# Changing the first feed-forward product of a two-layer attention network to a seven-product scheme, and moving the second bias into PSUM

## The chip, the cores and the metric

The kernel runs on one core of one Trainium2 chip. The metric is the device time of one execution in microseconds (us). One core has no second die to compare with, so the state of a run is told from its granted clock and from the spread of its times.

The engines are TensorE (PE, whose weight loads are listed as PEld), VectorE (DVE), ScalarE (ACT), GpSimd (POOL) and SyncE (SP, which here issues nearly all DMA).

## The reference

Two layers, each with windowed attention and a feed-forward part (FFN), over 2048 tokens of width 1024. The two layers use the same weights.

```python
def _A_ref(x, wqkv, wo):      # 32 heads of 32; each token sees 8 keys: itself and
    ...                       # those 2, 4, ... 14 positions back
    logits = jnp.einsum("bhsd,bhswd->bhsw", q, kg) * scale
    attn = _softmax(logits, axis=-1)
    o = jnp.einsum("bhsw,bhswd->bhsd", attn, vg)
    return o... @ wo
def _B_ref(x, w1, b1, w2, b2):    # w1 1024 x 3584, w2 3584 x 1024
    h = jnp.einsum("bsd,df->bsf", x, w1) + b1
    r = jnp.where(h > zero, h, zero)
    return jnp.einsum("bsf,fd->bsd", r * r, w2) + b2
for _ in range(2):
    x = x + _A_ref(_layernorm(x), A_wqkv, A_wo)
    x = x + _B_ref(_layernorm(x), B_w1, B_b1, B_w2, B_b2)
```

Inputs and weights are bf16; the only intermediate that matters here is `h`, which is formed by the first FFN product (FFN1).

## The kernel before

Tokens are worked in blocks of 512; four blocks and two layers make eight block steps, simply called blocks here. In each block PE does the q, k and v projections (`pq`), the output projection (`py`), FFN1 (`ph`), FFN2 (banks `X`, `Y`, `Z`) and a few sums over heads (`lg`). A small planner in the program orders the operations and assigns buffers; attention of the next block runs on DVE while PE does the FFN of this one.

FFN1 is plain: 28 output chunks of 8 matmuls with 512 columns each. ACT then takes the bank with bias and relu, and squares it.

```python
def SF1(self, u):
    for g in range(F // 512):
        wt = self.weights(self.w1_v[:, :, g * 512:(g + 1) * 512], KD)
        for cc in range(4):
            f = g * 4 + cc
            def fm(...):
                for kd in range(KD):      # KD = 8
                    nc.tensor.matmul(ph[:], wt[:, kd, cc * 128:(cc + 1) * 128], xnT[:, :, kd, :], start=(kd == 0), stop=(kd == KD - 1))
            def fr(...):
                nc.scalar.activation(out=r[:], in_=ph[:], func=ACTF.Relu, bias=self.b1T[:, f:f + 1], scale=1.0)
            def fs(...):
                nc.scalar.activation(out=r2[:, f, :], in_=r[:], func=ACTF.Square)
    ...
```

FFN2 already uses a seven-product scheme in three banks. Its combined weights (`tw`) are formed once on DVE in the first block and stored to DRAM; its raw weights come straight from the input `B_w2`. The bias b2 is added by DVE:

```python
# in SW, after the output projection and layernorm of each 128-token tile
nc.vector.tensor_tensor(xm[:], xm[:], self.b2b[:], ALU.add)
```

The softmax here doesn't subtract the row's maximum and nothing guards it: scores larger than these inputs give would overflow.

Of the kernel before, what the change touches and what calls it, by code (L numbers as in the profile page):

```python
# [15 lines left out]
W = 8  # L16
# [11 lines left out]
def dve(n, fast=True):  # L28
    return 0.15 + n * (0.000523 if fast else 0.00104)
# [170 lines left out]
class _Kernel:  # L200
# [19 lines left out]
    def setup(self):  # L220
        Buf.count.clear()
        nc, tc, ctx = self.nc, self.tc, self.ctx
        D, KF = self.D, self.KF
        const = ctx.enter_context(tc.tile_pool(name="const", bufs=1))
        nc.scalar.preload_act_table_set("natural_log_exp_and_others")
        self.ident = const.tile([128, 128], BF, name="ident")
        nc.vector.memset(self.ident[:], 1.0)
        nc.gpsimd.affine_select(out=self.ident[:], in_=self.ident[:], pattern=[[-1, 128]], compare_op=ALU.is_equal,
                                fill=0.0, base=0, channel_multiplier=1)
        self.grp = const.tile([128, H, 4], F16, name="grp")  # L230
        nc.vector.memset(self.grp[:], 1.0)
        nc.gpsimd.affine_select(out=self.grp[:], in_=self.grp[:], pattern=[[-4, H], [0, 4]], compare_op=ALU.is_ge,
                                fill=0.0, base=0, channel_multiplier=1)
        nc.gpsimd.affine_select(out=self.grp[:], in_=self.grp[:], pattern=[[4, H], [0, 4]], compare_op=ALU.is_ge,
                                fill=0.0, base=3, channel_multiplier=-1)
        self.mask01 = const.tile([128, W, HALO], F32, name="mask01")
        nc.vector.memset(self.mask01[:], 1.0)
        nc.gpsimd.affine_select(out=self.mask01[:], in_=self.mask01[:], pattern=[[-1, W], [1, HALO]],
                                compare_op=ALU.is_ge, fill=0.0, base=0, channel_multiplier=0)
        self.eps = const.tile([128, 1], F32, name="eps")  # L240
        nc.vector.memset(self.eps[:], EPS)
        self.b1T = const.tile([128, KF], F32, name="b1T")
        with nc.allow_non_contiguous_dma(reason="tiny bias load"):
            nc.gpsimd.dma_start(self.b1T[:], self.b1.rearrange("(c p) -> p c", p=128))
        self.b2b = const.tile([128, D], BF, name="b2b")
        nc.gpsimd.dma_start(self.b2b[:], self.b2.rearrange("(o d) -> o d", o=1).to_broadcast((128, D)))

        self.wqkv_v = self.wqkv.rearrange("(kt p) n -> p kt n", p=128)
        self.wo_v = self.wo.rearrange("(p c) n -> p c n", c=self.NCH)
        self.w1_v = self.w1.rearrange("(kt p) n -> p kt n", p=128)  # L250
        self.w2_v = self.w2.rearrange("(kt p) n -> p kt n", p=128)
        x2d = self.x if len(self.x.shape) == 2 else self.x.rearrange("b s d -> (b s) d")
        o2d = self.out if len(self.out.shape) == 2 else self.out.rearrange("b s d -> (b s) d")
        self.x_par = x2d.rearrange("(a two) d -> two a d", two=2)
        self.out_par = o2d.rearrange("(a two) d -> two a d", two=2)
        self.xs = [tc.dram_tile([self.S, D], F32, name=f"xs{l}") for l in range(self.n_layers - 1)]
        self.T = {"T1": 0, "T2": 1, "T3": 2, "T4": 3}
        self.B = {"B11": (0, 0), "B21": (1, 0), "B22": (1, 1)}
        self.tw = [tc.dram_tile([128, KF // 2, BLK], F16, name=f"tw{i}") for i in range(4)]
        self.xnd = [tc.dram_tile([self.S, D], BF, name=f"xnd{l}{h}") for l in range(self.n_layers) for h in "AB"]  # L260

        p = self.p
        self.arena = ctx.enter_context(tc.tile_pool(name="arena", bufs=1))
        self.psum = ctx.enter_context(tc.tile_pool(name="psum", bufs=1, space=PSUM))
        sizes = [("8K", 12, 8320), ("4K", 16, 4096), ("r2", 1, KF * BLK * 2), ("2K", 4, 2048), ("1K", 4, 1024),
                 ("H", 8, 128), ("s", 12, 32)]
        for c, n, b in sizes:
            p.classes[c] = (n, b)
        p.classes["ps"] = (8, 2048)
        p.caps.update(w=5, xt=2, P0=5, P1=5, pr=2, dn=1, pb=2, xm=8, xnA=1, xnB=1, s1=1, tw=4, xn=2, xo=2, q=1, k=1, v=1, o=1, e=1, r2=1)  # L270
# [12 lines left out]
    def dma(self, out, src, r, w, mb, prio=None, after=(), name="dma"):  # L283
        def fn():
            self.nc.sync.dma_start(out(), src())  # L285
        return self.p.add("SP", 0.08, fn, r, w, self.nxt() if prio is None else prio, after, mb=mb, name=name)
# [23 lines left out]
    def combine_group(self, j0, n):  # L310
# [3 lines left out]
        for k2 in range(2):  # L314
            for n2 in range(2):
                t = b[k2, n2] = Buf("4K", "tw", [128, step, BLK], F16)
                self.dma(lambda t=t, n=n: t[:, :n].bitcast(BF), lambda k2=k2, n2=n2, j0=j0, n=n: self.w2_block(k2, n2)[:, j0:j0 + n, :],
                         (), [(t, 0)], n * 0.131, name="twl")
# [25 lines left out]

    def ln(self, x, xv, xcells, xnT, tl, scr, key, prio, vec, on_pe=False):
        nc, p, D, KD = self.nc, self.p, self.D, self.KD
        xn = Buf("2K", "xn", [128, D], BF)
# [27 lines left out]
        else:  # L375
# [4 lines left out]
            def f2():  # L380
                nc.scalar.activation(out=xn[:], in_=xv(), func=ACTF.Square, bias=nmean(), scale=1.0, accum_out=s2())
                nc.scalar.activation(out=lnv(), in_=s2(), func=ACTF.Ln, bias=self.eps[:], scale=1.0 / D)
                nc.scalar.activation(out=rstd(), in_=lnv(), func=ACTF.Exp, scale=-0.5)
                nc.scalar.activation(out=nmr(), in_=nmean(), func=ACTF.Identity, scale=rstd())
            p.add("ACT", 1.3, f1, xr, [(xn, 0), (sm, 0)], prio, name="ln1")
            p.add("ACT", 1.8, f2, xr + [(sm, 0)], [(xn, 0), (sm, 1)], prio - 0.1, name="ln2")
# [10 lines left out]
    def ln_first(self, x, xv, xnT, tl):  # L397
        nc, p, D, KD = self.nc, self.p, self.D, self.KD
        xn = Buf("2K", "xn", [128, D], BF)
# [26 lines left out]
    def transpose(self, xn, xnT, tl, prio):  # L426
        nc, p, KD = self.nc, self.p, self.KD
        pt = Buf("ps", "pt", [128, KD, 128], BF)

        def f5():  # L430
            for kd in range(KD):
                nc.tensor.transpose(pt[:, kd, :], xn[:, kd * 128:(kd + 1) * 128], self.ident[:])

        def f6():
            nc.vector.tensor_copy(xnT[:, tl], pt[:])
        p.add("PE", 1.0, f5, [(xn, 0)], [(pt, 0)], prio, name="pt")
        p.add("DVE", 0.69, f6, [(pt, 0)], [(xnT, tl)], prio - 200.0, name="ptc")
# [12 lines left out]
    def SA(self, u):  # L450
        layer, b = divmod(u, self.NB)
        st = self.state.setdefault(u, {})
        xnT = Buf("8K", "xnA", [128, 4, self.KD, 128], BF)
# [11 lines left out]
    def SQ(self, u, jobs, order=None):  # L465
# [9 lines left out]
        for nm in jobs:  # L475
            st[nm] = Buf("8K", nm, [128, NCH, offs[nm] + BLK], F16)
# [12 lines left out]
        for nm, c0 in order:  # L489
# [3 lines left out]
            def fm(pq=pq, w=w, c0=c0):  # L493
                for kd in range(KD):
# [4 lines left out]
                  [(pq, 0)], [(dst, c0)], 2.0, name="cast")  # L499
# [7 lines left out]
    def S2(self, u, depths):  # L507
# [10 lines left out]
        def prod(hb):  # L518
# [5 lines left out]
            for c in range(NCH):  # L524
# [15 lines left out]
                if lvl == depth:  # L540
                    def fl(cur=cur, i=done):
                        for j in range(W // 2):
                            nc.tensor.matmul(lg[j][:], self.grp[:].rearrange("p h r -> p (h r)"), cur[:, 2 * j:2 * j + 2, :],  # L543
                                             start=(i == 0), stop=(i == nleaf - 1))
                    self.pe(4, fl, [(cur, 0)], [(g, 0) for g in lg], prio=-1.0, name="lg")
# [4 lines left out]
        def expo(hb):  # L550
            e = es[hb] = Buf("8K", "e", [128, W, HB], F32)
# [5 lines left out]
        def norm(hb):  # L557
            e = es[hb]
            t = Buf("4K", "dn", [128, W // 2, HB], F32)
            ri = Buf("1K", "ri", [128, HB], F32)  # L560
# [19 lines left out]
            p.add("DVE", dve(2048, False), f2, ec + [(ri, 0)], [(pb, 0)], self.nxt(), name="pb")  # L580

        def av(hb):
            pb = pbs[hb]
            for c in range(NCH):
# [10 lines left out]
                p.add("DVE", dve(1024) + dve(512) + dve(256), f2, [(pr, 0)], [(pr, 0), (o, (c, hb))], self.nxt(), name="avt")  # L595
# [10 lines left out]
    def SW(self, u):  # L606
# [5 lines left out]
        xnT = st["xnB"] = Buf("8K", "xnB", [128, 4, KD, 128], BF)  # L612
        wos = [self.weights(self.wo_v[:, :, g * 512:(g + 1) * 512], KD) for g in range(D // 512)]
        st["xm"] = []
        for tl in range(4):
            t = b * 4 + tl
            x, xv = self.load_x(layer, t, [st.get("gatek")])
            xm = Buf("4K", "xm", [128, D], F32)
            for db in range(D // 512):
# [7 lines left out]
                def fe(py=py, xm=xm, xv=xv, db=db):  # L627
# [5 lines left out]
                    (("xnd", 2 * layer + 1, t), 0), 1.0, True, on_pe=(u == 0))  # L633
            p.add("DVE", dve(1024, False), lambda xm=xm: nc.vector.tensor_tensor(xm[:], xm[:], self.b2b[:], ALU.add),
                  [(xm, 0), (xm, 1)], [(xm, 0), (xm, 1)], self.nxt(), name="b2")

    def SF1(self, u):
# [24 lines left out]

    def SF2(self, u):
# [17 lines left out]
        def mul(name, left, lcells, banks, start):  # L681
            for half in range(2):
                w = self.w2_rhs(name, half)
                for q in range(2):
                    def fm(w=w, q=q, half=half):
                        for j in range(g):
                            jj = half * g + j
                            nc.tensor.matmul(banks[q][:], left(jj, q), w[:, j, :], start=(start and jj == 0), stop=(jj == h - 1),  # L688
                                             skip_group_check=True)
                    self.pe(g, fm, lcells(half * g) + [(w, 0)], [(banks[q], 0)], name="pp")  # L690
# [24 lines left out]
        mul("B21", *block(1, 0), Y, True)  # L715
# [5 lines left out]
        mul("T1", lambda jj, q: s1[:, jj, q * 128:(q + 1) * 128], lambda j0: [(s1, j0)], Z, True)  # L721
# [11 lines left out]
        mul("T4", *block(1, 1), X, False)  # L733
# [15 lines left out]
    def build(self):  # L749
# [11 lines left out]
        for u in range(NU):  # L761
# [12 lines left out]
            self.SF1(u)  # L774
# [53 lines left out]
```

## Time and profile before

| | before |
|---|---|
| time, median of 15 runs (range) | 1235.25 us (1233.72 to 1237.5) |
| profiled span, granted clock | 1233.3 us, 0.997 |
| PE busy / idle | 1204.0 / 29.3 us |
| DVE, ACT busy | 962.2 us (78%), 614.5 us (50%) |
| DMA | 311.6 MB, 253 GB/s |

The prediction used three runs, with a median of 1236.23 us.

First, parts of the page of the kernel before: busy time by engine with its share of the span and the number of instructions, the chain of work that ended last, and the groups of FFN1. In a group line stand busy time, mean ns of one instruction, and the idle time of the engine just before them.

```profile
PE 1204.0 (98%) x5549; PEld 615.9 (50%) x5588; DVE 962.2 (78%) x1283; ACT 614.5 (50%) x1097; POOL 4.1 (0%) x10
...
PE 87%; DVE 7%; DMA 2%; SPq 2%; ACT 1%; issue 1%; ACTq 0%; DVEq 0%
...
L652 PE MATMUL ph<-xnB,w 128*128 128x512 bf16 x1792 | 389.4, 379 | 0.0
...
```

PE is the bound: it is busy 98% of the span and holds 87% of the chain. FFN1 is the largest group, 389 us, and PE never waits in it (0.0 us). The mean of 379 ns is the length of one pipelined matmul; the pace is found by dividing a stretch by its count, which gives 215.8 ns (146 matmuls issue in 31.5 us from 454.54).

The waits of PE in the kernel before (total us, times, longest) show what the idle time at the start is made of. `xn` is the output of layernorm; `pt` are its transposes on PE; `xnA` is the transposed input of the projections, brought by DMA from its copy `xnd` in DRAM; `w` is any weight buffer:

```profile
PE pt L432 <- ACT xn L418: 9.2, 3, 8.2
PE pq L496 <- DMA xnA<-xnd0A: 4.5, 1, 4.5
PE pt L432 <- ACT xn L352: 3.0, 4, 1.6
PE py L624 <- DVE o L593: 2.3, 1, 2.3
PE pq L496 <- DMA w<-in_A_wqkv_dram: 1.7, 1, 1.7
```

### The profile page before, as it was taken

What the parts mean: (1) busy time and instruction counts of PE and PEld (TensorE: products, weight loads), DVE (VectorE), ACT (ScalarE), POOL (GpSimd) and SP (SyncE); (2) the same over time, 40 slices, a digit from 0 to 9 for tenths busy, and PEclk for the clock granted to TensorE, in tenths of its full rate; (3) what the DMA queues carried; (4) which work ended last, traced back from release to release, by engine and by line L of the source; (5) the groups of instructions that cost most, each with busy time, mean ns of one, the idle gap of its engine ahead of it and who ended that gap; (6) DMA issues with size and microseconds to landing.
All of it is one profiled execution on the core that took longest, in us unless ns stands there. A gap on an engine that the chain in (4) does not pass through costs nothing.

```text
span 1233.3 us, 14702 instructions
## 1 busy us (share of the span) xinstructions
PE 1204.0 (98%) x5549; PEld 615.9 (50%) x5588; DVE 962.2 (78%) x1283; ACT 614.5 (50%) x1097; POOL 4.1 (0%) x10
## 2 busy tenths in 40 slices
PE   6988999999999999999999999999999999999998
PEld 3554544555445644456444564455544555444443
DVE  4999999998993989939897498957989399994032
ACT  6632793158901697027950379404892135721740
POOL 1000000000000000000000000000000000000000
PEclk9999999999999999999999999999999999999999
DMA  9776967977498874978759876697849976449915
GB/s 319 263 208 215 357 196 237 378 230 257 146 330 317 248 233 154 352 258 273 248 196 344 311 223 218 250 346 242 271 131 325 353 219 208 159 132 362 355 48 195
DMA packets 252327, 311.63 MB, mean 253 GB/s; under 512 B 69920, under 2 KB 197920, under 8 KB 252256
## 3 DMA queue, kind: packets, MB, share of 16 engines
q1 hardware_dynamic: 240512, 295.73, 71.3%
q10 hardware_dynamic: 8064, 14.68, 3.4%
q0 software_dynamic: 3680, 0.28, 0.5%
q8 instruction: 44, 0.72, 0.2%
q14 instruction: 27, 0.22, 0.0%
HBM read 261.36 MB, written 34.60 MB: 240 GB/s over the span
## 4 chain that ended last, share of the span: by engine, by line
PE 87%; DVE 7%; DMA 2%; SPq 2%; ACT 1%; issue 1%; ACTq 0%; DVEq 0%
PE ph L652 30%; PE pq L496 21%; PE X L688 15%; PE py L624 8%; PE Z L688 8%; PE Y L688 4%; SPq L285 2%; DVE pr L588 2%; PE lg L543 1%; DMA xt<-in_A_x_dram 1%; DVE P L528 1%; DVE pr L591 1%; DMA w<-tw 1%; DVE pr L592 1%; DVE tw L324 1%
## 5 line engine op out<-in xcount | busy, mean ns | idle before, releaser
L652 PE MATMUL ph<-xnB,w 128*128 128x512 bf16 x1792 | 389.4, 379 | 0.0
L496 PE MATMUL pq<-xnA,w 128*128 128x512 bf16 x1536 | 341.8, 382 | 7.0 <-DMA xnA<-xnd0A 4.5
L496 PEld LDWEIGHTS <-w 128*128 128x128 bf16 x1536 | 220.8, 144 | 123.2 <-issue 10.6
L652 PEld LDWEIGHTS <-w 128*128 128x128 bf16 x1792 | 175.4, 98 | 211.1
L688 PEld LDWEIGHTS <-r 128*128 128x128 f16 x1344 | 131.5, 98 | 159.5 <-issue 1.0
L688 PE MATMUL X<-w,r 128*128 128x512 f16 (+1 forms) x888 | 197.0, 379 | 1.2 <-DMA w<-tw 0.8
L655 ACT ACTIVATE r<-ph,b1T 128x512 f16<-128x512 f32 x224 | 152.1, 679 | 59.3 <-PE ph L652 53.9
L498 ACT CAST k<-pq 128x512 f16<-128x512 f32 x64 | 37.0, 588 | 286.5 <-PE pq L496 285.7
L528 DVE TENSOR_TENSOR P<-q,k 128x2048 f16<-128x2048 f16 x128 | 151.4, 1223 | 12.2 <-ACT q L498 12.2
L588 DVE TENSOR_TENSOR pr<-pb,v 128x2048 f16<-128x2048 f16 x128 | 156.4, 1222 | 0.6
L658 ACT ACTIVATE r<-r 128x512 f16<-128x512 f16 x224 | 141.0, 629 | 6.9
L536 DVE TENSOR_TENSOR P<-P,P 128x2048 f16<-128x2048 f16 x99 | 121.2, 1225 | 2.7
L624 PE MATMUL py<-w,o 128*128 128x512 bf16 x496 | 113.1, 383 | 3.1 <-DVE o L593 2.3
L591 DVE TENSOR_TENSOR pr<-pr 128x1024 f16<-128x1024 f16 x128 | 88.4, 690 | 3.8
L624 PEld LDWEIGHTS <-o 128*128 128x128 bf16 x512 | 50.4, 99 | 63.6 <-DVE o L593 2.9
L498 ACT CAST q<-pq 128x512 f16<-128x512 f32 x64 | 37.3, 583 | 41.8 <-PE pq L496 38.9
L592 DVE TENSOR_TENSOR pr<-pr 128x512 f16<-128x512 f16 x128 | 54.4, 425 | 4.4
L577 DVE TENSOR_TENSOR pb<-e,ri 128x2048 f16<-128x2048 f32 x16 | 36.7, 2291 | 26.3 <-ACT ri L574 26.3
L742 DVE TENSOR_TENSOR xo<-X,xm 128x512 f32<-128x512 f32 (+1 forms) x32 | 22.0, 688 | 43.4 <-PE X L688 41.9
L352 ACT ACTIVATE xn<-xm,sm 128x1024 bf16<-128x1024 f32 x32 | 39.7, 1242 | 32.2 <-DVE sm L370 32.2
L504 DVE COPY halo<-k 128x56 f16<-128x56 f16 x8 | 1.4, 177 | 68.7 <-ACT k L498 68.7
L679 DVE TENSOR_TENSOR s<-r 128x1792 f16<-128x1792 f16 x16 | 17.3, 1082 | 46.8 <-ACT r L658 46.8
(68 smaller groups left out, 820.3 us busy)
## 6 DMA issues: line engine op xcount, KB each, us to landing
w<-in_B_w_dram SPq DMA_DIRECT2D x56, 1024.0 KB, 8.1
w<-tw SPq DMA_DIRECT2D x64, 896.0 KB, 8.4
w<-in_A_wqkv_dram SPq DMA_DIRECT2D x48, 1024.0 KB, 9.7
w<-in_B_w_dram SPq DMA_DIRECT2D x48, 896.0 KB, 6.9
w<-in_A_wo_dram SPq DMA_DIRECT2D x16, 1024.0 KB, 9.0
xt<-xs SPq DMA_DIRECT2D x32, 512.0 KB, 9.1
xs<-xo SPq DMA_DIRECT2D x32, 256.0 KB, 6.7
xt<-in_A_x_dram SPq DMA_DIRECT2D x28, 256.0 KB, 7.5
```

The lines of the kernel that those rows point to most:

```text
L496: nc.tensor.matmul(pq[:], wv[:, kd % 4, c0:D:8], xnT[:, :, kd, :], start=(kd == 0), stop=(kd == KD - 1))
L498: p.add("ACT", act(512), lambda dst=dst, c0=c0, off=off, pq=pq: nc.scalar.copy(dst[:, c0, off:off + BLK], pq[:]), [(pq, 0)], [(dst, c0)], ...
L528: nc.vector.tensor_tensor(cur[:], q[:, c, None, hb * HB:(hb + 1) * HB].to_broadcast([128, W, HB]), _win_ap(k[:, c, :], HALO + hb * HB, HB) ...
L536: nc.vector.tensor_tensor(other[:], other[:], cur[:], ALU.add)
L588: nc.vector.tensor_tensor(pr[:], pb[:], _win_ap(v[:, c, :], HALO + hb * HB, HB), ALU.mult)
L591: nc.vector.tensor_tensor(pr[:, 0:4, :], pr[:, 0:4, :], pr[:, 4:8, :], ALU.add)
L592: nc.vector.tensor_tensor(pr[:, 0:2, :], pr[:, 0:2, :], pr[:, 2:4, :], ALU.add)
L624: nc.tensor.matmul(py[:], o[:, c, tl * 128:(tl + 1) * 128], wos[db][:, c, :], start=(c == 0), stop=(c == NCH - 1))
L652: nc.tensor.matmul(ph[:], wt[:, kd, cc * 128:(cc + 1) * 128], xnT[:, :, kd, :], start=(kd == 0), stop=(kd == KD - 1))
L655: nc.scalar.activation(out=r[:], in_=ph[:], func=ACTF.Relu, bias=self.b1T[:, f:f + 1], scale=1.0)
L658: nc.scalar.activation(out=r2[:, f, :], in_=r[:], func=ACTF.Square)
L688: nc.tensor.matmul(banks[q][:], left(jj, q), w[:, j, :], start=(start and jj == 0), stop=(jj == h - 1), skip_group_check=True)
```

## The change

The intent is to save PE work: FFN1 of blocks 2 to 8 is cut into 2 x 2 sub-blocks and computed with seven products in place of eight. A product is 8 matmuls of 256 columns. Seven products for each of seven steps make 392 matmuls of 256 columns in a block, where 224 of 512 stood. Half as many columns cost about half the time, so this is 7/8 of the work.

What pays for it:

- Combined weights. Seven groups of sums of w1 are formed on DVE during block 1 and stored to DRAM (`w1s`); blocks 2 to 8 load them, 7/4 as many bytes as plain w1.
- Combined activations: eight small DVE subtractions per block (`T`).
- Three PSUM banks per step (256 columns of the lower and 256 of the upper half of `h`; there are seven steps, worked two by two). Products 1, 6, 7 and 4 are summed one after another in bank X, and after each of the first three ACT must copy X away (`u`) before the next product may add to it. DVE then adds the copies to banks Y and Z, and adds bias and relu.
- To give DVE room, b2 moves into PSUM as a ones-by-b2 matmul inside FFN2 (6 per block, of 512 columns each), layernorm statistics move from DVE to ACT, and the softmax weights become bf16.

The diff also holds smaller matters: activations in f16 in place of bf16, differently cut buffer pools (14 of 4 KB in place of 16, for one), other priorities in the planner.

The diff, cut to its core:

```diff
-    def SF1(self, u):
+    def SF1_plain(self, u):        # kept for block 1
...
+    PAIR = [(0, 1), (1, 1), (0, 5), (1, 5), (0, 6), (1, 6), (0, 2), (0, 7), (1, 2), (1, 7), (0, 4), (0, 3), (1, 4), (1, 3)]
+    LAST = [(0, 1), (0, 5), (0, 2), (0, 6), (0, 7), (0, 4), (0, 3)]
+    def combine_w1_group(self, dp, after):
+        ...    # 4 raw loads, 4 DVE sums, 7 stores to self.w1s per group
+    def ffn1_step(self, r2, dp):
+        X, Y, Z = (Buf("ps", nm, [128, 2, HB], F32) for nm in "XYZ")
+        def keep(i):
+            p.add("ACT", act(512), lambda: nc.scalar.copy(us[i][:], X[:]), [(X, 0)], [(us[i], 0)], 1.0, name="u")
+        def mul(pr, w, wi, rhs, rc):
+            bank = {1: X, 6: X, 7: X, 4: X, 2: Y, 5: Z, 3: Z}[pr]
+            ...
+                for a in range(2):
+                    for k in range(4):
+                        nc.tensor.matmul(bank[:, a, :], lw[:, k, a * 128:(a + 1) * 128], rhs(k), ...)
+            ...    # 1, 6, 7: keep(); 2, 7, 3: DVE adds a copy to Y or Z, then bias and relu; square on ACT
...
-            p.add("DVE", ..., nc.vector.tensor_tensor(xm[:], xm[:], self.b2b[:], ALU.add), ...)
+                        if b2 is not None and half == 0:
+                            nc.tensor.matmul(banks[q][:], self.ones[:], self.b2r[:, b2 * BLK:(b2 + 1) * BLK], start=start, stop=False, ...)
...
-                    (("xnd", 2 * layer + 1, t), 0), 1.0, True, on_pe=(u == 0))
+                    (("xnd", 2 * layer + 1, t), 0), 1.0, False, on_pe=(u in (0, self.NU - 1)))
-            self.SF1(u)
+            (self.SF1 if u else self.SF1_plain)(u)
```

`PAIR` is the order in which the products of two steps are interleaved, as (step, product); `LAST` is the order of the seventh step, which stands alone.

## The prediction

> **What bounds it now.** TensorE. The page gives PE 1204.0 of 1233.3 us busy (98%) at granted clock 0.997. From the second of the eight token blocks on, the chain of waits is almost only matmuls; a block takes 147.6 us (FFN1 starts at 290.7, 438.3, 585.9 us): 192 pq + 64 py + 224 ph + 196 FFN2 + 8 lg = 684 matmuls of 512 columns, 0.2158 us each. Of the idle 29 us, 8 lie before the first transpose, 15 up to 133 us, 0.3 in each block. DVE is 78% busy, ACT 50%, DMA about 76%.
>
> **What changes.** FFN1 of blocks 2 to 8 becomes a seven-product (Strassen-like) scheme: per block 392 matmuls of 256 columns for 224 of 512.
>
> PE:
> - The Trainium skill ("TensorE: Matmul & The Clock Gate", Back-to-back issue gap) gives 262 cycles for 256 columns, 109 ns. The trace agrees as far as it can: eight 128-column transposes with their own weight loads issue some 57 ns apart, which with 215.8 ns at 512 interpolates to an estimated 110 ns. So weight loads should stay hidden. FFN1 goes from 48.35 to about 43.1 us: 7 x 5.2 = -36.6 us.
> - b2 moves from DVE into PSUM: 6 matmuls per block, 48 x 0.2158 = +10.4.
> - The last block's xnB is transposed on PE: 32 more, +2 to 3.
> - Net about -24 us, all on the critical path.
>
> DVE, per middle block (now 118.8 us busy in the stretch 382 to 530): removed b2 add 4.7, bn statistics about 7, pb in bf16 about 2. Added 21 adds out of PSUM at 0.69 (14.4; the skill, "VectorE: DVE Perf Modes", tier table: a PSUM operand keeps tensor_tensor at 1x, as 685 ns for xm shows), 28 small bias/relu (about 7), 8 half-block differences of 0.425 (3.4). Estimate 130 of 143 us. One-off: 28 weight combinations, about 19 us, in blocks 1 and 2.
>
> ACT: layernorm statistics move here, +2.8 us for each of 32 tiles; FFN1 epilogue 36.6 to about 33 per block.
>
> DMA: FFN1 weights per block from 7.2 to 12.8 MB in larger packets: that stretch goes from 190 to some 310 GB/s, about what FFN2 draws already (326 GB/s, with 0.3 us of PE idle). Forming the combinations adds 20 MB before about 290 us, where DMA is already 72 to 94% busy.
>
> **Critical path.** PE stays the bound, with little slack elsewhere: DVE has some 9 us per block before the next py waits for o; in FFN1 PE leaves ACT about 1.7 us to copy the X bank, and other ACT instructions take up to 1.25 us. I expect 0 to 1.5 us of new PE idle per block, and a few us near the start.
>
> **Prediction.** 1236 - 24 + 3 = **1215 us**, range 1200 to 1233. Chances: faster by over 2% (below 1211.5) 0.42, within 2% 0.55, slower 0.03.
>
> **What the profile would show.** Right: FFN1 matmuls 109 to 111 ns apart; steady block 143 to 145 us; PE 96% or more busy; DVE near 86%; the gain almost all in blocks 2 to 8. Wrong on the matmul: FFN1 well above 43 us with PEld near full. Wrong on slack: PE waiting in FFN1 for ACT copies or combined weights, or py for o.
>
> **What would make it wrong.** Weight loads not hidden at 256 columns; DMA saturation through FFN1 and FFN2; DVE falling behind; combined weights late for block 2. On the other side: less idle time at the start than now.

## More of the kernel before

Nearly all loads, the stores of results and the transposes of activations go into one SP queue (only the stores of layernorm outputs, `xnd`, are issued by ACT, and a few small loads by GpSimd); it works in order: a load whose buffer is not yet free holds up what stands behind it.

Next, the windows view of the kernel before. A line gives a stretch and its length in us, then the busy time of PE, PEld, DVE, ACT and POOL, the granted PE clock, the share of the 16 DMA engines' time that packets took (it can pass 1, since packets overlap), and GB/s. The first three lines split the run at the first output projection of block 2 and of block 7; the last three are FFN1, FFN2 and the projections of one middle block.

```profile
0.00:248.21 248.21, 224.05 (x1036) 120.99 (x1042) 222.23 (x299) 125.01 (x232) 4.08 (x10) 0.99 0.83 272
248.21:986.36 738.15, 736.83 (x3397) 378.74 (x3421) 594.56 (x787) 387.30 (x700) 0.00 (x0) 1.00 0.77 260
986.36:1233.30 246.94, 243.15 (x1120) 116.13 (x1127) 145.40 (x198) 102.20 (x165) 0.00 (x0) 1.00 0.64 210
438.20:487.70 49.50, 49.50 (x230) 22.44 (x230) 43.74 (x55) 45.63 (x82) 0.00 (x0) 1.00 0.60 191
487.70:529.80 42.10, 41.94 (x194) 19.16 (x195) 34.97 (x53) 1.63 (x3) 0.00 (x0) 1.00 0.93 329
529.80:585.80 56.00, 55.89 (x260) 34.08 (x260) 39.90 (x50) 30.11 (x57) 0.00 (x0) 1.00 0.78 264
```

Length less PE busy is PE's idle time: 24.2 us at the start, only 1.3 us over five whole blocks, 3.8 us at the end. So in the middle there is nothing to gain but PE work.

## The result, and the profile after

| | before | changed |
|---|---|---|
| time, median (range, runs) | 1235.25 us (1233.72 to 1237.5, 15) | 1233.3 us (1230.47 to 1236.18, 12) |
| profiled span, granted clock | 1233.3 us, 0.997 | 1233.8 us, 0.993 |
| PE busy / idle | 1204.0 / 29.3 us | 1183.9 / 49.9 us |
| DVE busy | 962.2 us (78%) | 1037.2 us (84%) |
| ACT busy | 614.5 us (50%) | 670.2 us (54%) |
| DMA | 311.6 MB, 253 GB/s | 368.2 MB, 298 GB/s |

The ratio to the kernel before is 0.9982, with a 95% interval of 0.997 to 0.9994. Ratios are the mean time of one kernel's fast runs over that of the other's of the same rounds, so they are not quite the ratios of the medians quoted. Executions over 1.5% slower than the fastest of the same kernel are left out of the means. The change gains about 2 us where 21 were forecast. The changed kernel's times fall into two groups, six from 1230.5 to 1232.6 us and five from 1235.5 to 1236.2, with one at 1234.0 between. The profiled run (1235.5) lies in the upper group, which is why the spans do not show even those 2 us. Why there are two groups is not known, and a wait seen in this one profile need not be in every run.

The page of the changed kernel, the same parts:

```profile
PE 1183.9 (96%) x6798; PEld 736.5 (60%) x6844; DVE 1037.2 (84%) x1556; ACT 670.2 (54%) x1240; POOL 4.0 (0%) x10
...
PE 70%; DVE 9%; ACT 9%; DMA 7%; SPq 2%; issue 1%; ACTq 0%; DVEq 0%
...
L787 PEld LDWEIGHTS <-w 128*128 128x128 f16 (+1 forms) x2520 | 246.3, 98 | 46.9 <-issue 10.3
...
L787 PE MATMUL X<-T,w 128*128 128x256 f16 x1120 | 137.5, 273 | 6.7 <-ACT u L761 6.6
...
L764 DVE TENSOR_TENSOR rr<-u,Z 128x512 f16<-128x512 f16 x98 | 65.2, 681 | 18.5 <-PE Z L787 10.2
```

PE's busy time fell by 20.1 us, and its idle time rose by 20.6 us. The chain of waits shows the same: PE has gone from 87% to 70%, and ACT and DMA have come in. L787 is the line of the seven-product matmuls, L761 the ACT copy of bank X.

The windows view of the changed kernel, cut at the same events; the last three lines are 4 us stretches around one stall and are used further down:

```profile
0.00:254.04 254.04, 226.10 (x1041) 121.47 (x1047) 221.89 (x304) 136.38 (x256) 4.01 (x10) 0.97 1.01 322
254.04:986.35 732.31, 719.04 (x4261) 463.03 (x4290) 645.11 (x976) 419.61 (x785) 0.00 (x0) 1.00 0.92 308
986.35:1233.80 247.45, 238.81 (x1498) 152.02 (x1507) 170.20 (x276) 114.23 (x199) 0.00 (x0) 0.99 0.70 246
443.50:489.50 46.00, 43.37 (x385) 37.37 (x384) 43.13 (x75) 40.62 (x73) 0.00 (x0) 1.00 0.99 302
489.50:534.40 44.90, 44.16 (x213) 21.01 (x214) 42.01 (x63) 4.37 (x7) 0.00 (x0) 1.00 0.98 347
534.40:590.50 56.10, 55.99 (x260) 34.14 (x261) 43.04 (x59) 39.16 (x78) 0.00 (x0) 1.00 0.73 251
236.00:240.00 4.00, 1.51 (x8) 0.78 (x6) 3.93 (x7) 0.00 (x0) 0.00 (x0) 1.00 1.06 357
240.00:244.00 4.00, 4.00 (x13) 1.72 (x11) 3.83 (x7) 0.70 (x2) 0.00 (x0) 0.57 1.15 297
244.00:248.00 4.00, 4.00 (x20) 2.63 (x19) 3.86 (x7) 1.65 (x3) 0.00 (x0) 1.00 1.02 330
```

From the first three lines of both kernels comes the account that the rest of this document explains:

| stretch | PE busy, before to after | forecast for it | PE idle, before to after | length |
|---|---|---|---|---|
| start, to the first py of block 2 | 224.1 to 226.1 (+2.0) | +1.3 (b2) | 24.2 to 27.9 (+3.8) | +5.8 |
| five blocks, to the first py of block 7 | 736.8 to 719.0 (-17.8) | 5 x (-5.2 + 1.3) = -19.7 | 1.3 to 13.3 (+12.0) | -5.8 |
| the rest | 243.2 to 238.8 (-4.3) | -10.5 + 2.6 + 2.5 = -5.4 | 3.8 to 8.6 (+4.9) | +0.5 |

The waits of PE in the changed kernel:

```profile
PE pt L495 <- ACT xn L481: 9.4, 3, 8.1
PE pq L559 <- DMA xnA<-xnd0A: 8.9, 1, 8.9
PE X L787 <- ACT u L761: 6.6, 9, 1.3
PE pq L559 <- DMA w<-in_A_wqkv_dram: 4.1, 2, 2.5
PE X L787 <- DMA w<-w1s: 2.5, 1, 2.5
PE Y L842 <- DMA w<-in_B_w_dram: 2.3, 3, 1.0
PE X L842 <- DMA w<-in_B_w_dram: 2.2, 1, 2.2
PE pt L495 <- ACT xn L412: 2.0, 3, 1.0
PE lg L606 <- DVE P L599: 1.3, 2, 1.1
```

No single new wait explains the whole. At the start the waits for xnA and wqkv by DMA rose by 4.4 and 2.4 us, while others fell. In FFN1 of blocks 2 to 7 and at its joint with FFN2 there are 6.6 us of waits for the ACT copy, 2.5 for combined weights and 4.5 for raw FFN2 weights.

The timeline of the changed kernel (start, duration, instruction; in brackets the idle time before it and what ended it; SPq and ACTq are the instructions with which SyncE and ACT issue DMA) shows the pace of the matmuls, a queue that stands still, and the two kinds of waits for the copy:

```profile
442.70 9.73 SPq L457 DMA_TRANSPOSE xnA<-xnd1A  x2
...
451.23 1.91 PE L787 MATMUL X<-T,w 128*128 128x256 f16 x16
452.97 1.04 PE L787 MATMUL X<-xnB,w 128*128 128x256 f16 x8
...
777.55 1.04 PE L787 MATMUL X<-T,w 128*128 128x256 f16 x8
778.63 0.59 ACT L761 CAST u<-X 128x512 f16<-128x512 f32 x1
779.26 1.03 PE L787 MATMUL X<-T,w 128*128 128x256 f16 x8 [0.67 <-ACT u L761]
...
924.67 0.42 ACT L636 ACTIVATE dn<-dn 128x256 f32<-128x256 f32 x1 [0.76 <-DVE dn L633]
925.12 0.42 ACT L637 ACTIVATE ri<-dn 128x256 bf16<-128x256 f32 x1
925.44 0.57 ACT L761 CAST u<-X 128x512 f16<-128x512 f32 x1
926.06 1.03 PE L787 MATMUL X<-T,w 128*128 128x256 f16 x8 [1.19 <-ACT u L761]
```

- Sixteen matmuls issue in 1.74 us (451.23 to 452.97), or 109 ns each: the forecast pace.
- At 777.55 PE's product into X ends at 778.59, the copy begins 0.04 us later and takes 0.59, and the next X product has stood idle for 0.67 us. Here ACT was just free: its last squares ended at 778.60. This is the bare length of the chain product, copy, product. It appears in the seventh step, which has no second step beside it, between products 6 and 7 in blocks 2, 5 and 7 (in block 6 it is longer, see below); in blocks 3, 4 and 8 the planner put FFN2 matmuls between these two products, and no wait for the copy is listed. The product that should start at 778.42 (8 x 109 ns after 777.55) starts at 779.26, so the price is 0.84 us: 0.67 idle, and about 0.17 that the page counts as busy. That fits the listed length of one such matmul, 273 ns: it is 164 ns more than the pace of 109, an overlap that is lost when PE stands.
- At 924.67 ACT is at the head of its queue with a softmax reciprocal that itself waits 0.76 us for DVE. The copy stands behind it and starts at 925.44, 0.56 us after its product's end at 924.88; PE waits 1.19 us.
- At 442.70 the SP queue stands for 9.73 us at two transposes. The next load of combined weights is issued at 452.48 only, and at 467.24 PE waits 2.5 us for weights.

### The profile page after: what moved, and what is told of

The parts are those of the page before. It is cut to its first block, busy times and chain, and to the rows that moved or that the text cites. A ratio compares the mean times of both kernels' runs of the same rounds, so it can differ in the third digit from the quotient of the medians.

```text
span 1233.8 us, 17891 instructions
## 1 busy us (share of the span) xinstructions
PE 1183.9 (96%) x6798; PEld 736.5 (60%) x6844; DVE 1037.2 (84%) x1556; ACT 670.2 (54%) x1240; POOL 4.0 (0%) x10
## 4 chain that ended last, share of the span: by engine, by line
PE 70%; DVE 9%; ACT 9%; DMA 7%; SPq 2%; issue 1%; ACTq 0%; DVEq 0%
PE pq L559 17%; PE X L842 12%; PE X L787 10%; PE py L687 7%; PE Z L842 6%; PE Z L787 5%; DMA w<-in_B_w_dram 4%; PE ph L713 4%; PE Y L842 3%; PE Y L787 2%; DVE pr L651 2%; SPq L291 2%; ACT xn L412 2%; ACT xn L441 1%; ACT xn L437 1%
## 5 line engine op out<-in xcount | busy, mean ns | idle before, releaser
L559 PE MATMUL pq<-xnA,w 128*128 128x512 f16 x1536 | 344.2, 384 | 13.8 <-DMA xnA<-xnd0A 8.9
L559 PEld LDWEIGHTS <-w 128*128 128x128 bf16 x1536 | 220.6, 144 | 132.6 <-issue 17.4
L787 PEld LDWEIGHTS <-w 128*128 128x128 f16 (+1 forms) x2520 | 246.3, 98 | 46.9 <-issue 10.3
L787 PE MATMUL X<-T,w 128*128 128x256 f16 x1120 | 137.5, 273 | 6.7 <-ACT u L761 6.6
L775 ACT ACTIVATE r<-rr 128x1024 f16<-128x1024 f16 x98 | 101.9, 1059 | 11.3 <-DVE rr L771 9.3
L761 ACT CAST u<-X 128x512 f16<-128x512 f32 x147 | 83.8, 591 | 38.7 <-PE X L787 35.4
L692 DVE TENSOR_TENSOR xm<-py,xt 128x512 f32<-128x512 f32 x64 | 43.7, 689 | 51.3 <-PE py L687 49.0
L764 DVE TENSOR_TENSOR rr<-u,Z 128x512 f16<-128x512 f16 x98 | 65.2, 681 | 18.5 <-PE Z L787 10.2
L655 DVE TENSOR_TENSOR pr<-pr 128x512 f16<-128x512 f16 x128 | 54.4, 425 | 4.4
L803 ACT ACTIVATE rr<-X,b1T 128x256 f16<-128x256 f32 x98 | 41.9, 471 | 23.5 <-PE X L787 22.3
L842 PE MATMUL Y<-w,r 128*128 128x512 bf16 x218 | 51.3, 379 | 2.5 <-DMA w<-in_B_w_dram 2.3
```

Of the source, the lines that this page charges most:

```text
L559: nc.tensor.matmul(pq[:], wv[:, kd % 4, c0:D:8], xnT[:, :, kd, :], start=(kd == 0), stop=(kd == KD - 1))
L655: nc.vector.tensor_tensor(pr[:, 0:2, :], pr[:, 0:2, :], pr[:, 2:4, :], ALU.add)
L761: p.add("ACT", act(512), lambda: nc.scalar.copy(us[i][:], X[:]), [(X, 0)], [(us[i], 0)], 1.0, name="u")
L764: p.add("DVE", dve(512, False), lambda: nc.vector.tensor_tensor(r[:, :, m, :], us[i][:], bank[:], ALU.add), [(us[i], 0), (bank, 0)], [(r, ...
L775: p.add("ACT", act(1024), lambda: nc.scalar.activation(out=r2[:, f:f + 2, :].rearrange("p a t -> p (a t)"), in_=r[:].rearrange("p a m t -> ...
L787: nc.tensor.matmul(bank[:, a, :], lw[:, k, a * 128:(a + 1) * 128], rhs(k), start=(start and k == 0 and a == 0), stop=(k == 3), skip_group_ ...
```

## The experiments

Three explanations were set against each other first. The first, D, is bandwidth: FFN1 and FFN2 both draw 300 to 350 GB/s now, so weights come late. The second, Q, is the single in-order SP queue that stands still. The third, E, is the in-order ACT queue, behind which the X copies stand. Where the expectations use letters, they mean these. That DVE was too full was a further candidate.

All were run three rounds (four runs of each, with the kernel before on the same chip). The medians of before were 1235.16, 1235.66, 1235.88 and 1235.07 us in the four sets. "Better" without more means than the 1233.3 us of the changed kernel; where a difference of 2 or 3 us is at stake, recall that the changed kernel itself ranges over 6 us, in two groups. Traces are of one run each.

### Set 1: bytes

**half_w1s.** Half the bytes of the combined weights are loaded; the number and order of loads stay. The result is wrong.

```diff
-  self.dma(lambda w=w, n=n: w[:, 0:n], lambda ...: self.w1s[d0 // 2][:, j:j + n], ...
+  self.dma(lambda w=w, n=n: w[:, 0:n, 0:2], lambda ...: self.w1s[d0 // 2][:, j:j + n, 0:2], ...
-  nc.tensor.matmul(bank[:, a, :], lw[:, k, ...
+  nc.tensor.matmul(bank[:, a, :], lw[:, k % 2, ...
```

> Wrong result on purpose: each load of combined FFN1 weights brings half the bytes (two of four K tiles, used twice), 6.4 MB less per block; every engine's instructions and their order are unchanged. Theory D (the DMA engines are saturated through FFN1 and FFN2, so weights land late): the 3 to 3.7 us of PE idle in each of blocks 2 to 8 go, FFN1+FFN2 of a middle block falls from 90.9 to about 87.5 us, the steady block from 147.0 to about 143.5, time 1210 to 1218. Theory Q (the SP queue issues loads late because it stands behind DMA transposes that wait for their stores; bytes don't matter): 1228 to 1233. Theory E (PE waits for ACT's copies and for banks in FFN1): 1230 to 1233.

Measured: 1231.88 us (1229.27 to 1233.65), ratio 0.9972 [0.9956, 0.9989]. That is about 1.4 us better than the changed kernel, and within its spread; the waits for the ACT copy stayed at 6.6 us. The bytes that the change adds to FFN1 are therefore not the main cause.

**few_combos.** The DMA of four of the seven groups of combinations is left out at the start; later loads read an already formed group in their place. The result is wrong.

```diff
+        real = dp not in (2, 3, 4, 5)     # loads and stores of the other groups become nothing
-  lambda ...: self.w1s[d0 // 2][:, j:j + n],
+  lambda ...: self.w1s[d0 // 2 * (d0 == 6)][:, j:j + n],
```

> Wrong result on purpose: for four of the seven weight groups the loads and stores that form the combinations are left out (11.5 MB less before 300 us), the VectorE work of forming them stays, the order stays; blocks read another group's combinations instead, as many bytes as before. Theory D: the loss of 5.8 us up to the start of FFN1 of block 2 (296.5 against 290.7 us) shrinks to 1 to 2 us, steady blocks stay at 146 to 147 us, time 1228 to 1230. If the start is lost to the VectorE work of the combinations or to the order instead: FFN1 of block 2 still starts at 295 to 297 us and the time stays at 1232 to 1234.

Measured: 1228.97 us (1227.46 to 1231.24), ratio 0.9955 [0.9938, 0.9971], 4.3 us better than the changed kernel. The first py of block 2 starts at 247.60 us, for 254.04 in the changed kernel and 248.21 before. The traffic of forming the combinations is the cause of the net loss at the start. The longer wait for xnA is not part of it, for it is still there:

```profile
PE pq L567 <- DMA xnA<-xnd0A: 8.8, 1, 8.8
```

It was made up again early: the first FFN1 product of block 1 starts at 139.9 us in the changed kernel and at 140.4 before. The loss lies behind that point, where four waits of the changed kernel between 215 and 240 us (0.68, 0.21, 0.90 and 2.49 us) are gone in few_combos.

**half_and_few.** Both edits together (wrong).

```diff
+        real = dp not in (2, 3, 4, 5)
+  self.w1s[d0 // 2 * (d0 == 6)][:, j:j + n, 0:2]
```

> Both of the edits above together. Theory D: the forecast of the matmul arithmetic comes true, 1206 to 1213 us, steady block 143 to 144 us, PE idle in all about 30 us as before the change. Theories Q and E: at most 6 us below the changed kernel, 1227 or more.

Measured: 1226.45 us (1225.47 to 1227.96), ratio 0.9931 [0.9916, 0.9946]: 6.9 us better, about the sum of the two. With both edits the kernel moves 311.7 MB, as much as the kernel before. All the added bytes together are thus worth some 7 us, a third of what was missing. D as the main cause has fallen.

**no_b2_matmul.** The 48 b2 matmuls are left out. (The outputs lack b2; b2 is so small that they still pass the comparison.)

```diff
-                        if b2 is not None and half == 0:
+                        if False:
-  start=(start and jj == 0 and b2 is None)
+  start=(start and jj == 0)
```

> Wrong result on purpose: the 48 matmuls that add b2 are left out of FFN2 (10.4 us of PE work), all else and the order stay. If PE sets the pace there: 1222 to 1224 us. Theory D: FFN1 and FFN2 take as long as their bytes take, so PE only idles more; the gain is 0 to 4 us, 1229 to 1233, and a middle block stays at 146 us or more.

Measured: 1225.14 us (1224.25 to 1226.53), ratio 0.992 [0.9905, 0.9935]: 8.2 us better, where the PE time taken out is 48 x 0.2158 = 10.4 us. So most of the PE work is still on the critical path, and PE remains the bound. The new waits come on top of PE's work.

### Set 2: queues

**act_thin.** ACT's work is made shorter: squares become copies of half as many elements, and layernorm statistics run over 128 columns only. The number of instructions stays. The result is wrong.

```diff
-  nc.scalar.activation(out=xn[:], in_=xv(), func=ACTF.Square, bias=nmean(), ...
+  nc.scalar.activation(out=xn[:, 0:128], in_=xv()[:, 0:128], func=ACTF.Square, bias=nmean(), ...
-  nc.scalar.activation(out=r2[...], in_=r[...], func=ACTF.Square)
+  nc.scalar.copy(r2[...].bitcast(F32), r[...].bitcast(F32))
```

> Wrong result on purpose: in the changed kernel ScalarE's squares become f32 copies of half as many elements, and the two statistics passes of each layernorm read 128 of 1024 columns; order and DMA bytes unchanged. The halved-bytes run moved the time by only 1.4 us and left the listed PE waits for ACT's u copies at 6.6 us, so theory E is now the leading one: PE stands where an in-order ACT has squares or layernorm passes ahead of the copy of X. Theory E: those waits fall from 6.6 us to under 2 and the time to 1223 to 1228. Theory Q (SP queue) or D (bytes): 1231 to 1234.

Measured: 1227.38 us (1226.0 to 1228.86), ratio 0.9933 [0.9918, 0.9948], 6 us better. The waits of PE in this run:

```profile
PE X L787 <- ACT u L761: 3.9, 5, 1.2
```

They were 6.6 us in 9 waits. Most of the waits behind other ACT work went; what stayed is the bare chain, four waits of 0.67 us, and one of 1.18. The time fell by more than these 2.7 us. In the trace, the wait of 2.5 us for combined weights in block 3 is gone too, and the first py of block 2 starts 1.6 us earlier; how ACT's work leads to these was not tested. ACT's squares and layernorm passes also stand in the kernel before, which was not run with this edit, so not all of the 6 us need be a cost of the change.

**pool_issue.** The loads of combined weights are issued by GpSimd, in a queue of its own, to test Q.

```diff
-            self.nc.sync.dma_start(o if cast is None else o.bitcast(cast), src())
+            eng = self.nc.gpsimd if name == "wf" else self.nc.sync
+            eng.dma_start(o if cast is None else o.bitcast(cast), src())
```

> Changed kernel with the loads of combined FFN1 weights issued by GpSimd instead of SP, same bytes and same order otherwise, right result. Theory Q (loads of FFN1 and of the first FFN2 weights are issued late because SP stands at a transpose or at a busy buffer): the 2.5 us wait for w in block 3 and the waits for the first raw w2 tiles (2 to 4 us in all) go, 1226 to 1230. If lateness comes from the transfers themselves: 1231 to 1236.

Measured: 1301.67 us (1280.66 to 1323.18), ratio 1.0435 [1.0352, 1.0518]; its profiled run was slow, with a clock of 0.97, so only its waits are read here, as a sign and not as a size:

```profile
PE Y L788 <- DMA w<-w1s: 25.5, 3, 14.5
PE X L788 <- DMA w<-w1s: 13.4, 4, 5.4
```

Weights came later, not earlier. The Trainium skill says of the issuing engine ("DMA: Bandwidth & Descriptors", Issuing engines are not separate DMA queues) that all issuing engines end on the same 16 DMA engines, and that issuing on several at once saves only sequencer time. The two fast runs, 1280.66 and 1298.28 us, lie 47 and 65 us above the changed kernel, so there was nothing to win here; that the engines are shared is not shown by it. It is a different path, so the run says nothing for or against Q.

**smooth_v.** The v projections of the next block are interleaved with FFN1, so that PE does other work while ACT copies X.

```diff
+                np_ += 1
+                if np_ % 5 == 2:
+                    next(fill, None)       # one chunk of the v projection
...
-                self.SQ(u + 1, "v")
+                (generator handed to SF1)
```

> Changed kernel with the eight v projections of the next block spread among the FFN1 products instead of standing before them (right result): FFN1's load on ACT and DMA is spread over some 57 us instead of 43. Theories E and D both say fewer waits: 1220 to 1229. If the waits come from neither (the order alone): 1231 or more.

Measured: 1256.03 us (1253.84 to 1259.86), ratio 1.0168 [1.0148, 1.0187]: a miss. The waits for u rose from 6.6 to 15.5 us and those for combined weights from 2.5 to 5.8. A likely reason, not tested alone, is that the v projection brings its own ACT copies (586 ns in the median) and its own weight loads into the same two queues.

**before_more_bytes.** The kernel before, with three quarters of each FFN1 weight tile loaded a second time, to give it the bytes of the change without its arithmetic.

```diff
+            load = self.p.ops[-1]
+            if u:
+                def again(wt=wt, g=g, first=load.fn):
+                    first()
+                    nc.sync.dma_start(wt[:, 0:6, :], self.w1_v[:, 0:6, g * 512:(g + 1) * 512])
+                load.fn = again
```

> Kernel before, with three quarters of each FFN1 weight tile loaded a second time in blocks 2 to 8 (12.8 MB per block, as the changed kernel loads), right result, no other change. Theory D in its strong form (these bytes alone make PE starve): 10 to 20 us over the kernel before. After the halved-bytes run I expect less: 0 to 5 us over it, 1235 to 1240.

Measured: 1255.68 us (1251.43 to 1260.84), ratio 1.0166 [1.0132, 1.0201]. The run is confounded, as the waits of the SP queue show:

```profile
SPq L649 <- DMA w<-in_B_w_dram: 319.1, 49, 9.0
```

The second load goes into the same tile, and the queue waited for the first to land each time, 319 us in all. It adds bytes and makes the queue stand, and can't tell which of the two cost the 20 us. What the bytes alone cost is to be read from half_w1s.

### Set 3: parts of the change

**last_first.** The seventh step, whose chain lies bare, is done first, when ACT is less loaded.

```diff
-        for d0 in range(0, self.NDP, 2):
+        for d0 in [6, 0, 2, 4]:
```

> Changed kernel, right result, one line: the unpaired seventh group of FFN1 products is computed first instead of last, so that products of the pairs can stand between its four uses of one X bank. Theory E in the form of a dependency chain (product into X, ACT copy of X, next product into X; some 0.84 us lost each time nothing stands between, at the end of FFN1 in four to six blocks): 1227 to 1230. If ACT's load counts and not that chain: 1232 to 1235.

Measured: 1246.67 us (1244.05 to 1247.75), ratio 1.0086 [1.0069, 1.0103]: a miss. The reason stands in its waits:

```profile
PE X L787 <- DMA w<-w1s: 14.0, 1, 14.0
```

That step's combinations are formed last, so block 2 waited for them. The steady block, from one start of FFN1 to the next, did not gain (146.4 us; the changed kernel has 147.0, 147.0, 145.5 and 146.5, the kernel before 147.6, and 143 to 145 were forecast).

**b2_on_dve.** The bias b2 goes back to DVE, where it was; the rest of the change stays. Correct.

```diff
+            p.add("DVE", dve(1024, False), lambda xm=xm: nc.vector.tensor_tensor(xm[:], xm[:], self.b2r[:], ALU.add), ...
-                        if b2 is not None and half == 0:
+                        if False:
```

> One part of the change undone, right result: b2 is added by VectorE again (1.2 us for each of 32 tiles, 4.8 us per block) and the 48 matmuls go. Leaving those matmuls out alone gave 8 us. If VectorE has the 9 us of slack per block that the prediction counted: 1224 to 1228. If VectorE at 91% has none: 1230 to 1236.

Measured: 1227.72 us (1226.77 to 1230.19), ratio 0.994 [0.9921, 0.9959]. This is the best correct version, faster than before by 0.6% and 5.6 us below the changed kernel. DVE is busy 1070.1 us (87%), and no wait of PE for DVE over 1 us appears. So DVE had room, and moving b2 to PE was a loss.

**plain_f1.** FFN1 goes back to the plain product in all blocks; the rest of the change stays. Correct.

```diff
-            (self.SF1 if u else self.SF1_plain)(u)
-            if u == 0:
+            self.SF1_plain(u)
+            if False:                      # no combinations
```

> The seven-product FFN1 undone in all blocks, with its combinations, all other parts of the change kept (right result). PE work is then that of the kernel before plus 10.4 us of b2 and some 2 us of transposes. If these parts cost what they occupy on PE: 1245 to 1250, and the seven-product scheme alone brings 12 to 17 us of its 36.6. If layernorm statistics on ACT or the smaller pools cost more: over 1252. If they cost nothing: 1236 to 1240, and the scheme itself brings next to nothing.

Measured: 1258.44 us (1257.84 to 1259.26), ratio 1.0185 [1.017, 1.02]. The rest of the change, without the seven-product scheme, costs about 22.5 us: 10.4 of it is the b2 matmuls by their count, and nearly half of what remains is in this wait (3.0 us before, for the same kind of instruction):

```profile
PE pt L495 <- ACT xn L412: 8.6, 3, 4.0
```

The scheme itself, taken as the changed kernel less this one, brings 25 us of the 36.6 that were forecast for it; that counts 6.6 us of the wait above, which is only 2.0 us in the changed kernel.

**all_thin.** The edits of act_thin and half_and_few together (wrong): if the causes found are separate, they should add.

```diff
+  (the diffs of act_thin and half_and_few together)
```

> Wrong result on purpose: the thin ACT work, the halved FFN1 weight bytes and the left-out combination traffic together. If the three are separate losses that add up (6.0 + 1.4 + 4.3 us): 1220 to 1223. If each hides part of the others: 1208 to 1216, close to the 1212 that the PE work alone would give. If they overlap: 1224 or more.

Measured: 1220.42 us (1218.73 to 1222.41), ratio 0.9877 [0.9861, 0.9893]: 12.9 us better than the changed kernel. The parts add to 6.0 + 1.4 + 4.3 = 11.7. The windows of this run, cut at the same events as above:

```profile
0.00:245.97 245.97, 222.79 (x1046) 121.53 (x1047) 218.20 (x298) 120.31 (x256) 4.00 (x10) 0.98 0.93 290
245.97:970.88 724.91, 719.41 (x4291) 463.31 (x4290) 647.69 (x983) 338.75 (x785) 0.00 (x0) 1.00 0.83 265
970.88:1217.00 246.12, 238.84 (x1509) 152.20 (x1507) 170.17 (x276) 91.74 (x199) 0.00 (x0) 0.99 0.60 196
```

The idle time of the five blocks fell from 13.3 to 5.5 us with PE busy unchanged (719.0 and 719.4). At the start it fell from 27.9 to 23.2. At the end only from 8.6 to 7.3.

### Set 4: the chain, and a better version

**last_order.** Product 2, which goes to bank Y, is moved in the seventh step to stand between products 6 and 7. Correct.

```diff
-    LAST = [(0, 1), (0, 5), (0, 2), (0, 6), (0, 7), (0, 4), (0, 3)]
+    LAST = [(0, 1), (0, 5), (0, 6), (0, 2), (0, 7), (0, 4), (0, 3)]
```

> Changed kernel, right result, one line: in the unpaired seventh group of FFN1, product 2 (bank Y) moves from before to behind product 6, so that it stands between products 6 and 7, which both use bank X. Dependency chain: the stalls of 0.67 us idle (0.84 with the pipe's refill) at the end of FFN1 in blocks 2, 5, 6 and 7 go, 2 to 5 us, 1228 to 1231. If they come from ACT's load: no change, 1232 to 1235.

Measured: 1230.62 us (1228.38 to 1231.98), ratio 0.9963 [0.9948, 0.9978]. All four runs lie within or below the lower group of the changed kernel's times, so the 2.7 us are not a sure gain. Nor did the edit do what it says in every block: the planner places operations itself, and in blocks 2, 5, 7 and 8 it still ran product 2 (into Y) before product 6, as here in block 5:

```profile
773.77 1.04 PE L787 MATMUL Y<-xnB,w 128*128 128x256 f16 x8
774.65 1.04 PE L787 MATMUL X<-T,w 128*128 128x256 f16 x8
776.36 1.03 PE L787 MATMUL X<-T,w 128*128 128x256 f16 x8 [0.67 <-ACT u L761]
```

In blocks 2, 5 and 7 the 0.67 us stall is still there. In block 6 product 2 did run between 6 and 7, and the stall of 1.19 us is gone; the reciprocal also came after the copy there, so that block alone proves little. But over both traces the order goes with the wait: it stands in every block where 7 follows 6 directly, and is not listed in any where another product lies between. About 2 us came at the start (first py of block 2 at 252.03), which the edit was not meant to touch.

**b2_dve_order.** The two correct edits b2_on_dve and last_order together.

```diff
+  (the diffs of b2_on_dve and last_order together)
```

> Right result: b2 on VectorE again (alone 1227.7) and the new order of the seventh group. If separate: 1223 to 1226. If VectorE, now some 3% fuller, takes over as the late one: 1227 or more.

Measured: 1228.86 us (1227.88 to 1231.9), ratio 0.9955 [0.994, 0.997]. They do not add; this is b2_on_dve within its spread. In block 7 product 2 now ran between 6 and 7, but product 4 followed 7 directly, and the 0.67 us came there.

**b2_dve_from3.** In addition, the scheme starts at block 3, to spread the forming of the combinations.

```diff
-            (self.SF1 if u else self.SF1_plain)(u)
-            if u == 0:
+            (self.SF1 if u > 1 else self.SF1_plain)(u)
+            if u == 1:
```

> Right result: the same, with the seven-product FFN1 only from block 3 on and the combinations formed over twice the time. The loss at the start (4.3 us by few_combos) should go, the gain of block 2 (2 to 3 us as measured) is given up: 1 to 2 us below b2_dve_order, 1222 to 1225. If forming the combinations later starves other loads instead: above b2_dve_order.

Measured: 1240.43 us (1238.04 to 1241.3), ratio 1.0047 [1.003, 1.0064]: a miss. One block's saving is given up, and the start did not get shorter (first py of block 2 at 258.2).

**b2_dve_uprio.** In addition to b2_dve_order, the planner gives the X copies the highest rank on ACT.

```diff
-  [(X, 0)], [(us[i], 0)], 1.0, name="u")
+  [(X, 0)], [(us[i], 0)], -5.0, name="u")
```

> Right result: as b2_dve_order, with ACT's copies of X given the highest priority when the static order is made. If queueing behind layernorm passes and reciprocals matters: 1 to 3 us below b2_dve_order. If the order was made with the copy not yet ready, priority changes nothing much: within 1.5 us of it.

Measured: 1229.55 us (1227.62 to 1230.76), ratio 0.9955 [0.994, 0.997]: no change. A likely reason is that a rank only orders what the planner believes to be ready; it does not shorten the ACT instruction that is running, nor the chain.

## Why the prediction was wrong, and where it was right

**Right: the bound and the matmul.** PE was and is the bound: taking 10.4 us of matmuls away brought 8.2. The Trainium skill ("TensorE: Matmul & The Clock Gate", Back-to-back issue gap) gives 262 cycles for 256 columns, and the trace agrees: 109 ns, with 98 ns weight loads hidden behind them (PEld rose from 50 to 60% busy, and FFN1 is not held by it).

**Nearly right: PE work.** Forecast -24 us, measured -20.1 us busy. "b2 moves ... +10.4" is confirmed by no_b2_matmul. The 3.9 us that are missing are not more matmuls but time that stalls cause and that the page counts as busy. Two parts can be seen. The stall measured above costs about 0.17 us beyond its idle time. And after some stalls the clock falls: in the windows above, the 2.49 us wait that ends at 239.35 is followed by 4 us at a granted clock of 0.57, in which 13 matmuls are counted, and then 20 in the next 4 us. The clock seems to be the larger part: by the windows view PE worked for about 12 us at half clock in the changed kernel (after the waits that end at 77.57, 239.35 and 1080.22) and for about 7 us in the kernel before (after those that end at 73.82 and 114.01), which by these numbers is an estimated 2.5 us of longer busy time. How the 3.9 us divide was not tested.

**Right: DVE.** "DVE has some 9 us per block": b2_on_dve put about 33 us of work back on DVE (1037.2 to 1070.1), and the time fell. The skill's figure for adds out of PSUM ("VectorE: DVE Perf Modes", tier table: `tensor_tensor` at 1x with any PSUM operand) agrees with 681 ns for 512 columns, where an f16 add of 512 columns with no operand in PSUM takes 425 (L655). The same room made the b2 move unneeded; the other helper moves were not undone alone.

**Wrong: the idle time.** The step that failed is "I expect 0 to 1.5 us of new PE idle per block, and a few us near the start", entered in the sum as +3 us. Measured was +20.6 us: +3.8 at the start, +12.0 in five blocks (2.4 per block; by its length the stretch fell 13.9 us short of the forecast, 2.8 per block), +4.9 at the end. The prediction named each of the causes as a risk: ACT's copy of X, DMA through FFN1 and FFN2, combined weights late near the start. It then gave all of them together 3 us. For the copy it set one ACT instruction of 1.25 us against 1.7 us of room. But the copy needs 0.59 us of that room itself; ACT does two squares in a row (2.00 us from 776.60), or a reciprocal that waits for DVE; and in the seventh step of four blocks nothing stands between products 6 and 7 into X. What the runs showed in its place:

| cause | shown by | worth |
|---|---|---|
| X copies behind other ACT work (squares 1.06 us, layernorm passes 1.06 to 1.24 us, a reciprocal waiting for DVE): 2.7 us in the trace; the way of the rest is open | act_thin | 6.0 us |
| forming the combined weights while DMA is already full at the start | few_combos | 4.3 us |
| more weight bytes in FFN1 of blocks 2 to 8 | half_w1s | 1.4 us, near the spread |
| all three | all_thin | 12.9 us |

About 17.6 us of idle time were unforeseen, and experiments that thin the suspected work won back 12.9 us of time (not all of it need be the change's share, since the kernel before was not thinned in the same way). For the rest there is the trace alone. Even in all_thin, 5.5 us of idle time remain in the five blocks and 7.3 at the end. The changed kernel's end has a 2.2 us wait for the first raw FFN2 weights, 1.1 us for `lg`, and one 0.67 us chain; each is seen in the waits, none was taken away alone. The bare chain (0.84 us in the seventh step) rests on the timelines, on act_thin leaving it unchanged, and on the order of products in last_order; an edit that fills the gap in every block was not run. Whether the SP queue, which stands at transposes and at loads whose buffers are not free, causes the late FFN2 weights is open: pool_issue failed as a test.

**Where the sum went.** 1236 - 24 + 3 = 1215 became, by the profiled spans, 1233.3 - 20.1 + 20.6 = 1233.8. The prediction's gain was real PE work saved; nearly every microsecond of it came back as PE waiting, in pieces of 0.2 to 2.5 us, in the blocks and behind the forming of the combined weights. The gain forecast for "blocks 2 to 8" appears in five of them in part (-5.8 us) and not in the last two, where +4.9 us of idle eats it.

**The range.** 1200 to 1233 just failed to hold 1233.3. The prediction gave its largest chance, 0.55, to a time within 2%, and that is what came; this was more luck than insight, for the idle term of its sum was 3 us and the measured one 20.6.

## What to carry to other kernels

When an engine is 98% busy, taking work from it moves the kernel into the many small waits that its work had covered: size these from the longest instruction that can stand in front of the new one in each in-order queue, not from the average busy share. A scheme that cuts the flops but makes several products accumulate in one bank, with a copy between them, puts the copy's full length (here 0.67 us idle, 0.84 in all) on the path wherever no independent product is left to fill it. Ask of every helper move ("to give DVE room") whether the room was needed: undoing that one alone gave the best correct kernel, 1227.7 us.

## What the Trainium skill lacked or had wrong

- "TensorE: Matmul & The Clock Gate", Back-to-back issue gap, calls about 131 ns per matmul at 512 columns the sustained figure and 216 ns the isolated one. Long streams with a weight load for each matmul run at 215.8 ns at 512 columns, and at 109 ns at 256: here the "isolated" formula is the sustained pace.
- The same page, Part 1: The HAM clock gate, says that the clock falls after an idle window of about 3.4 us, on a free-running window. Here a wait of 2.49 us was already followed by 4 us at 0.57, while another of 2.50 us (ending at 467.24) was followed by a granted clock of 1.00. In the kernel before, a wait of 2.26 us (ending at 114.01) was followed by 0.50 from 115 to 118. That fits a free-running window, but a limit of 3.4 us for a single gap is too generous.
- No page that was read gives the length of the chain PE product, ACT copy out of PSUM, PE product into the same bank: 0.67 us of idle for 128 x 512, of which 0.59 is the copy.
- "HBM Reference" says that a core streaming alone measures well above the share of about 358 GB/s. The trace agrees in a single stretch of 4 us, with 426 GB/s (463 to 467); over a whole FFN2 of a middle block it was 347 GB/s with DMA 98% busy.
- No page that was read, "DMA: Bandwidth & Descriptors" among them, gives a figure for what it costs a whole kernel to move a set of large loads from SyncE to GpSimd. Here it took the time from 1233.3 us to 1280.66 and 1298.28 us in the two fast runs.
